# A hand-written step list after its first 43 steps in another order (attention into a GELU layer, 1 core)

## The chip, the cores and the metric

One core of one Trainium2 chip. The metric is the device time of one launch in microseconds (us); lower is better. The kernel runs alone on its core, and the granted TensorE clock is 1.000 throughout the profiled execution.

## The reference

The first half is a cross-covariance attention over channels, the second a GELU layer on its output. Cut to what matters:

```python
# q, k, v: (4, 6080, 256) float32; w_in (256, 2048), w_out (2048, 256)
qn = q / (norm(q, axis=1) + 1e-06)
kn = k / (norm(k, axis=1) + 1e-06)
s = kn.transpose(0, 2, 1) @ qn / tau        # 256 x 256 for each of 4 batches
a = softmax(s)
x = (v @ a).reshape(24320, 256)
h = x @ w_in
g = gelu_tanh(h)
out = g @ w_out
```

## The kernel before

The product `a @ w_in` is formed once for each batch (`AW`), so that the tokens need only `v @ AW`, the GELU and `@ w_out`. The tokens are cut into 48 blocks of up to 512 (12 for each batch, the twelfth of each batch has 448). All work beyond a first stretch for batch 0 is cut into small steps, and the order of these steps is written out by hand: `ORDER` is a list of 48 strings, the program walks through it from left to right, and each step puts its instructions at the end of the in-order queue of its engine. A step `M5A-2` in string n works on block n-2; no step is moved by a scheduler.

What the steps of one block n are:

- `g0`..`g7` (TensorE, L521) multiply v by a pair of column blocks of AW into a PSUM tile `h` that is one of two pairs of banks; `G0`..`G7` (ScalarE, L531) apply the GELU to it and write bfloat16. Four matmuls of 512 columns for each `g`.
- Up to three *sets* w0, w1, w2 replace two such pairs each by seven half-size products (a Strassen-Winograd scheme): `w0m1`..`w0m7` on TensorE (`small`, L604, two matmuls of 256 columns each) write two PSUM tiles, `qp` (which shares the two pairs of banks with `h`) and `rb`. Between them stand `w0y5` (ScalarE, L623, copies half of `qp` to SBUF), `w0cq` (ScalarE, L620, copies `rb` into the other half of `qp`), `w0ap` and `w0ax` (VectorE, L625 and L628, sums of `rb` and that copy), and three GELUs `w0Gq`, `w0Gr`, `w0Gx` (L630, L635, L638). `w0m6` adds to `rb` and so waits for `w0cq`; `w0m3` and `w0m7` wait for `w0ap`; `w0m4` waits for `w0ax`.
- The second layer is a Winograd scheme as well: `M1A`, `M1B` to `M7A`, `M7B` (TensorE, `product`, L736, four matmuls of 256 columns each) accumulate in the halves r and p of one PSUM tile `rp`, of which there is one. `T1a`, `T2`, `T3`, `T4` (VectorE) are the sums of g that M5, M6, M7 and M4 read. `y5` (ScalarE, L759) copies p to SBUF, then `cq` (ScalarE, L794) copies r to p, and M2 and M6 go on from there; then `c11` (VectorE, L774) transposes r into the output tile, `ap` (VectorE, L798) writes p plus the copy into r, and M3 and M7 go on; `ax` (L765) reads p before M4; `c12` and `c21` read both halves before M1 of the next block.
- In between lies the attention of the next batch: `lq`, `lk`, `lv` (loads on GpSimd's queue, each behind the last matmul issued so far), `lt` (a transposing load on SyncE's queue, which also holds the stores), `row0`.. (TensorE, L253), `qsq`, `ksq` (squares, on ScalarE or for some on VectorE, L192 and L194), `f1`..`f3`, `sp`, `sa`, and the chain from `gc` to the copies `ac0`..`ac7` and the sums `SW0`..`SW2` for the sets. `pF0`, `pS1` and the like prepare `w_out` once, early.

So within one block there are two places where ScalarE reads half of a PSUM tile and writes the same tile (`y5` and `cq` of the block, `y5` and `cq` of each set) and one where VectorE does (`c11` and `ap`). The pairs as the code writes them, the block's first, then the set's (`hc` is half the block's columns, `c` all of them):

```python
elif what == "y5":    # keep(): SBUF <- ACCS[n, "p"], on nc.scalar
    keep(n, "p", "y5")
elif what == "cq":
    nc.scalar.activation(ACCS[n, "p"][:, :hc], ACCS[n, "r"][:, :hc], AF.Copy)
...
if what == "cq":
    nc.scalar.activation(qp(n, i)[:, 0, :c], RB[n, i][:, :c], AF.Copy)
if what == "y5":
    YW[n, i] = set_buffer(n, i, "y")
    nc.scalar.activation(YW[n, i][:, :c], qp(n, i)[:, 1, :c], AF.Copy)
```

Of the kernel before, what the change touches and what calls it, by code (L numbers as in the profile page):

```python
# [18 lines left out]
def kernel(  # L19
# [1004 lines left out]
    """g0 lq+2 w2m4-1 w1ax-1 w1m4-1 row1-1 w1Gr-1 c11-2 ap-2 M3A-2 T4-2 M3B-2 sp-2 sa-2 vs M7A-2
    M7B-2 ax-2 w2Gr-1 G0 w0m1 w0m5 w0cq w0y5 row2-1 g3 G3 w0m6 c12-2 row0 ksq-1 w0ap f1-1 M4B-2
    M4A-2 c21-2 row3-1 w1m5 w0m7 w1Gx-1 lk+2 w1y5 w1m1 w1cq w0m2 w0m3 w0Gq w0ax w0Gx T2-1 M1A-1
    M5B-1 w1m6 w1ap w0m4 w0Gr M1B-1 T4-1 w2m5 w2y5 M5A-1 y5-1 cq-1 w1m7 w2m1 w2cq w1m2 row4 w1m3
    w1Gq M6B-1 w1ax M2B-1 w1m4 M2A-1 vs+1 M6A-1 T3-1 w2m6""",
    """w0m5 w1Gr-1 row3-1 row5-3 w0m1 w1Gx-1 row4-3 ksq-1 c11-2 ap-2 M7A-2 w0cq w0y5 M7B-2 w2ap-1
    c22-3 w2m3-1 w2m2-1 w2m7-1 w2Gq-1 qsq+1 f2-2 f3-2 w2ax-1 row2-1 w0m6 w0ap M3B-2 M3A-2 c12-2  # L1030
    ax-2 lk w2Gx-1 w2m4-1 w2Gr-1 row2-3 g0 G0 lt+2 T1a-1 T2-1 w0m7 qsq-1 w0m2 w0m3 M4A-2 row0-3
    M4B-2 c21-2 lv+3 w0ax sp-2 sa-2 g3 M1A-1 G3 w0Gq c22-2 f1-1 M1B-1 M5A-1 M5B-1 y5-1 T3-1 f2-1
    cq-1 row1-1 w1m1 w1m5 w0m4 w2m5 w1cq w0Gr T4-1 row0+1 M6B-1 w1y5 w1m6 M6A-1 w2m1 M2A-1 M2B-1
    w2y5 w0Gx w1ap w1m3 w1m2 w1m7 f3-1 row3+1 w2cq w2m6 row2+1 qsq c11-1 ap-1 M3B-1 M7A-1 w1ax
    w1m4 w1Gx w1Gq w2ap M7B-1 ax-1 w1Gr ksq row1 w2m7 w2m3 w2m2 lk+6 w2ax M3A-1 w2Gq M4B-1 w2Gx
    vs+1 w2m4 sp-1 sa-1 lt+3 M4A-1 c21-1 row2 row5-1""",
# [4 lines left out]
    """w0m1 vs c11-2 w1m7-1 g7-1 G7-1 ap-2 M3A-2 w1ax-1 lt+2 w0m5 T1a-1 w0cq M7A-2 M7B-2 M3B-2 f1-1
    w0y5 ax-2 w0m6 w0ap w1m4-1 g0 w1Gx-1 M4B-2 T2-1 w1Gr-1 w0m7 w0ax row4-1 f2-1 lv+3 w0m3 G0
    w0m2 M4A-2 w0Gq w1m1 c12-2 w1m5 c21-2 w1cq row5-1 w1y5 w0m4 w0Gr row4-4 row1-1 gc M1A-1 w0Gx
    w1m6 M1B-1 f3-1 T4-1 w1ap M5B-1 M5A-1 vs+1 w2m5 y5-1 sp-1 sa-1 pow w1m2 w1m3 T3-1 w1m7 cq-1
    M6A-1 lv+4 lt+3 M2B-1 M2A-1 M6B-1 w1Gq w1ax w2y5 w2m1 w2cq w1m4 w1Gr c11-1 ap-1 kf kr c22-2
    g3 G3 w2m6 M7B-1 w2ap M7A-1 ax-1 krp lq+4""",
    """w0m1 S1 S0 w2m7-1 T1a-1 w1Gx-1 w0m5 w0cq w0y5 w2m3-1 M4A-2 lq+4 w2m2-1 w2Gq-1 M4B-2 w2ax-1
    w0m6 th1 th0 w0ap M3A-2 c22-2 M3B-2 c12-2 c21-2 w2Gx-1 w2m4-1 g0 dn w0m7 w0m3 w0m2 T2-1
    M1B-1 rc3 w2Gr-1 lt+3 G0 M1A-1 M5A-1 M5B-1 rc1 g3 w0Gq g4 w0ax y5-1 cq-1 G3 T3-1 rc2 G4
    M2B-1 w1m1 w1m5 rc0 M6B-1 w0m4 M6A-1 w1cq w1m6 w1y5 w1ap lk+4 ksq+3 M2A-1 g7 w1m7 w0Gx c11-1  # L1050
    ap-1 w1m2 w1m3 M7A-1 eT M3A-1 w0Gr w1Gq w1ax lv+4 G7 vs+1 M7B-1 rsum+1 rs+1 w1m4 M3B-1""",
# [19 lines left out]
    w2m6 w1ax w1m4 w1Gr w1Gx M7B-1""",
    """w0m5 M3A-2 w0m1 T4-2 w0cq w2ap-1 T1a-1 ax-2 w2m3-1 w2m2-1 w2m7-1 row4+2 w2Gq-1 w2ax-1 ksq
    row0-1 w0y5 w0m6 w0ap M4A-2 w2Gx-1 M4B-2 w2m4-1 w2Gr-1 c21-2 g3 w0m7 G3 c12-2 lt+2 w0m2 w0m3
    M1B-1 M5B-1 M5A-1 w0Gq w0ax w0Gx w0m4 T2-1 vs+1 w0Gr T4-1 w1m1 w1m5 row0+2 w1cq lv+3 M1A-1
    row4-2 sp-2 sa-2 row5-2 y5-1 cq-1 w1y5 w1m6 w1ap w2m5 w2y5 M6B-1 w2m1 w2cq M6A-1 M2B-1
    row1-2 f1-1 f2-1 qsq row3-1 w2m6 w2ap w1m3 w1m2 w1Gq w1m7 w1ax w1Gx M2A-1 c11-1 ap-1 lv+6
    f3-1 row1+2 w2m3 w2m7 w2ax w1m4 w1Gr T3-1 w2m2 w2Gq g0 M3A-1 G0 M3B-1 w2Gx c12-1 c22-2 lt+3""",
    """g3 G3 w0m5 w0m1 T1a-1 T2-1 M7B-2 w2m4-1 M7A-2 ax-2 w0y5 w0cq g0 w2Gr-1 w0m6 w0ap row0-3 row1
    row3+1 sp-2 sa-2 f1-1 G0 qsq M4B-2 M4A-2 c21-2 c22-2 lk+2 w1m5 w1y5 w1m1 w0m7 w0m3 w0ax w0m2
    M1B-1 M5B-1 vs+1 w1cq w1m6 w0Gq w1ap w0Gx w0m4 w0Gr M1A-1 M5A-1 y5-1 cq-1 w2m5 w1m7 w1m3  # L1080
    w1m2 T3-1 w2m1 w2y5 w2cq M2A-1 w1Gq w1ax M6B-1 w1m4 T4-1 w1Gr w2m6 w2ap lt+4 w1Gx lk+3 M6A-1
    M2B-1""",
    """w0m5 w0y5 w0m1 w0cq w2m3-1 w2m2-1 c11-2 ap-2 f2-2 w2m7-1 row5 w2Gq-1 M3A-2 w0m6 w2ax-1
    w2Gx-1 M3B-2 f3-2 w0ap row5-1 w2m4-1 M7A-2 ksq-1 w0m7 M7B-2 w0ax w2Gr-1 ax-2 g0 qsq c12-2
    lq+1 vs+1 w0m4 w0Gr row0-2 w0m2 T1a-1 w0m3 lq+2 M4A-2 M4B-2 c21-2 G0 sp-2 row3-1 w1m1 w1m5
    row3-2 row2-1 f1-1 w0Gq M1A-1 M1B-1 f2-1 f3-1 w1cq sa-2 w1m6 M5A-1 M5B-1 row4-1 sp-1 w2m5
    w1y5 w1ap ksq c22-2 lt+2 w1m3 w1m2 w1m7 sa-1 y5-1 cq-1 w2m1 M2B-1 M2A-1 T2-1 M6A-1 M6B-1
    lk+3 T3-1 w1Gq w0Gx g3 w2y5 w2cq w2m6 w1ax w1m4 w1Gx row5-2 w1Gr row3+1 G3 c11-1 ap-1 M7B-1
# [193 lines left out]
```

## Time and profile before

| | us |
|---|---|
| median of 3 runs | 697.04 |
| lowest, highest | 696.74, 697.15 |
| the profiled execution, its own time | 696.96 |
| its span, first to last instruction | 695.2 |

Outside the span lie 1.76 us (696.96 less 695.2). The views are read so: a *page* has busy times by engine and the costliest groups of instructions; the *chain* is the work that ended last, followed back from the end, and its pieces give a start, a length and a count of instructions; the *timeline* gives each instruction's start and length in us, with equal neighbours merged under a count (x4). The length of a matmul in the trace is modelled and is longer than the distance to the next one's start, so holds of TensorE are read from starts. PE is TensorE, PEld its weight loads, ACT ScalarE, DVE VectorE, POOL GpSimd, SP SyncE.

### The profile page before, as it was taken

What the parts mean: (1) busy time and instruction counts of PE and PEld (TensorE: products, weight loads), DVE (VectorE), ACT (ScalarE), POOL (GpSimd) and SP (SyncE); (2) the same over time, 40 slices, a digit from 0 to 9 for tenths busy, and PEclk for the clock granted to TensorE, in tenths of its full rate; (3) what the DMA queues carried; (4) which work ended last, traced back from release to release, by engine and by line L of the source; (5) the groups of instructions that cost most, each with busy time, mean ns of one, the idle gap of its engine ahead of it and who ended that gap; (6) DMA issues with size and microseconds to landing.
All of it is one profiled execution on the core that took longest, in us unless ns stands there. A gap on an engine that the chain in (4) does not pass through costs nothing.

```text
span 695.2 us, 14706 instructions
## 1 busy us (share of the span) xinstructions
PE 677.7 (97%) x5707; PEld 543.8 (78%) x5707; DVE 630.0 (91%) x1111; ACT 624.0 (90%) x945; POOL 74.5 (11%) x135
## 2 busy tenths in 40 slices
...
GB/s 241 207 270 133 180 151 115 110 118 69 151 128 117 110 90 144 131 115 94 173 83 132 95 110 132 64 107 101 46 92 61 117 77 85 99 47 64 70 62 58
DMA packets 161463, 79.08 MB, mean 114 GB/s; under 512 B 148449, under 2 KB 152161, under 8 KB 160673
## 3 DMA queue, kind: packets, MB, share of 16 engines
...
## 4 chain that ended last, share of the span: by engine, by line
PE 82%; ACT 8%; DVE 4%; DMA 4%; issue 1%; DVEq 0%; POOL 0%; ACTq 0%; POOLq 0%
PE rp L736 36%; PE h L521 15%; PE rb L604 13%; PE qp L604 10%; PE G L253 4%; DMA t<-in_k_dram 3%; PE awp L454 1%; DMA t<-in_q_dram 1%; ACT g L531 1%; ACT yw L623 1%; ACT qp L620 1%; ACT g L635 1%; ACT sq L192 1%; PE o L748 1%; ACT g L630 1%
## 5 line engine op out<-in xcount | busy, mean ns | idle before, releaser
L736 PEld LDWEIGHTS <-wcomb 128*128 128x128 bf16 x2632 | 256.0, 98 | 43.9 <-issue 2.4
L736 PE MATMUL rp<-t,wcomb 128*128 128x256 bf16 (+1 forms) x1504 | 209.3, 272 | 0.1
L736 PE MATMUL rp<-g,wcomb 128*128 128x256 bf16 (+1 forms) x1128 | 160.2, 272 | 0.3 <-ACT rp L794 0.2
L531 ACT ACTIVATE g<-h 128x1024 bf16<-128x1024 f32 (+1 forms) x136 | 137.6, 1017 | 11.6 <-PE h L521 11.0
L630 ACT ACTIVATE g<-qp 128x1024 bf16<-128x1024 f32 (+1 forms) x124 | 125.0, 1015 | 9.3 <-PE qp L604 8.8
L521 PE MATMUL h<-vT,aw 128*128 128x512 bf16 (+1 forms) x456 | 115.8, 377 | 0.2 <-ACT g L630 0.2
L604 PEld LDWEIGHTS <-sw 128*128 128x128 bf16 x992 | 96.3, 98 | 23.9 <-issue 2.4
L625 DVE TENSOR_TENSOR qp<-rb,yw 128x512 f32<-128x512 f32 (+1 forms) x124 | 85.3, 689 | 13.0 <-PE rb L604 5.3
L604 PE MATMUL rb<-tv,sw 128*128 128x256 bf16 (+1 forms) x496 | 93.0, 271 | 0.4
L628 DVE TENSOR_TENSOR xw<-rb,yw 128x512 f32<-128x512 f32 (+1 forms) x124 | 83.4, 675 | 2.0 <-PE rb L604 1.3
L521 PEld LDWEIGHTS <-aw 128*128 128x128 bf16 x544 | 52.8, 98 | 39.2 <-DVE aw L362 0.6
L604 PEld LDWEIGHTS <-aw 128*128 128x128 bf16 x744 | 72.4, 98 | 13.3 <-issue 0.2
L620 ACT ACTIVATE qp<-rb 128x512 f32<-128x512 f32 (+1 forms) x124 | 71.9, 583 | 8.3 <-PE rb L604 2.9
L638 ACT ACTIVATE g<-xw 128x512 bf16<-128x512 f32 (+1 forms) x124 | 77.4, 627 | 1.7 <-DVE xw L628 1.5
L635 ACT ACTIVATE g<-rb 128x512 bf16<-128x512 f32 (+1 forms) x124 | 72.7, 595 | 3.6 <-PE rb L604 3.2
L623 ACT ACTIVATE yw<-qp 128x512 f32<-128x512 f32 (+1 forms) x124 | 73.0, 596 | 2.4 <-PE qp L604 0.7
L192 ACT ACTIVATE sq<-t 128x1536 bf16<-128x1536 bf16 (+4 forms) x49 | 64.5, 1335 | 6.2 <-DMA t<-in_q_dram 6.0
L774 DVE STREAM_TRANSPOSE ot<-rp 128x256 f32<-128x256 f32 (+1 forms) x141 | 59.0, 433 | 6.2 <-PE rp L736 5.2
L253 PE MATMUL G<-t 128*128 128x256 bf16 (+1 forms) x352 | 60.6, 277 | 0.6 <-DMA t<-in_k_dram 0.6
L711 DVE TENSOR_TENSOR t<-g,t 128x2048 bf16<-128x2048 bf16 (+1 forms) x47 | 56.7, 1207 | 0.5
L707 DVE TENSOR_TENSOR t<-g,t 128x2048 bf16<-128x2048 bf16 (+1 forms) x47 | 56.3, 1198 | 0.5
L709 DVE TENSOR_TENSOR t<-g 128x2048 bf16<-128x2048 bf16 (+1 forms) x47 | 56.5, 1203 | 0.0
...
## 6 DMA issues: line engine op xcount, KB each, us to landing
...
vb<-in_v_dram POOLq DMA_DIRECT2D x41, 256.0 KB, 4.2
t<-in_q_dram POOLq DMA_DIRECT2D x21, 384.0 KB, 6.0
t<-in_k_dram POOLq DMA_DIRECT2D x21, 384.0 KB, 5.9
...
```

Of the source, the lines that this page charges most:

```text
L253: nc.tensor.matmul(G[b][:, jc, :], lhsT=qt[:np_, r, jc * 128 : jc * 128 + 128], rhs=kt[:np_, r, :], start=first and jc == 0, stop=jc == 1, ...
L521: mm = nc.tensor.matmul(hp[:, u, :cols], lhsT=AW[b][:, cc, fc * 128 : fc * 128 + 128], rhs=vt_tiles[n][:, cc, :cols], start=cc == 0, stop= ...
L531: nc.scalar.activation(gs(n)[:, 2 * p : 2 * p + 2, :cols], HP.pop((n, p))[:, :, :cols], AF.Gelu_apprx_tanh)
L604: GATE[0] = nc.tensor.matmul(acc[:, u * hc : u * hc + hc], lhsT=lhs[:, u * 128 : u * 128 + 128], rhs=rhs, start=m in (1, 5) and u == 0, st ...
L620: nc.scalar.activation(qp(n, i)[:, 0, :c], RB[n, i][:, :c], AF.Copy)
L623: nc.scalar.activation(YW[n, i][:, :c], qp(n, i)[:, 1, :c], AF.Copy)
L625: nc.vector.tensor_add(qp(n, i)[:, 1, :c], RB[n, i][:, :c], YW[n, i][:, :c])
L628: nc.vector.tensor_add(XW[n, i][:, :c], RB[n, i][:, :c], YW.pop((n, i))[:, :c])
L630: nc.scalar.activation(gs(n)[:, 2 * pa : 2 * pa + 2, :c].rearrange("p u (t x) -> p t u x", t=2), QP.pop((n, i))[:, :, :c].rearrange("p t ( ...
L635: nc.scalar.activation(gs(n)[:, 2 * pb : 2 * pb + 2, :hc], two(RB.pop((n, i))[:, :c]), AF.Gelu_apprx_tanh)
L638: nc.scalar.activation(gs(n)[:, 2 * pb : 2 * pb + 2, hc:c], two(XW.pop((n, i))[:, :c]), AF.Gelu_apprx_tanh)
L736: nc.tensor.matmul(ACCS[n, acc][:, :hc], lhsT=wcomb[:, w, fc, :], rhs=x, start=first and k == 0, stop=k == 3, skip_group_check=True)
```

## The change

The list `ORDER` is replaced from its 44th step on (the first string, 38 steps, and five steps of the second stay). All 3887 steps are the same ones, with the same tiles and shapes and so the same instructions; only their sequence differs, and with it where the 48 strings are cut. Of the diff, the early part and two strings:

```diff
-    """g0 vtr0-1 vtr1-1 lt+2 lv+3 G0 g3 G3 M1A-1 g2 lq+1 G2 g1 pF0-1 lk+1 lt+3 pS1-1 G1 pA12-1
-    M1B-1 M5B-1 M5A-1 g6 g7 pF1-1 pS2-1 T3-1 y5-1 cq-1 M2B-1 T2-1 M6A-1 M6B-1 pS4-1 vs+1 M2A-1
-    c11-1 ap-1 row5 G6 G7 pNA-1 g5 pS3-1""",
+    """g0 vtr0-1 vtr1-1 lt+2 lv+3 pF0-1 M1A-1 g3 G0 SW1-1 lq+1""",
+    """w0m1 G3-1 pS1-2 g2-1 G2-1 M1B-2 T2-2 pA12-2 g1-1 G1-1 M5A-2 M5B-2 y5-2 cq-2 g6-1 pF1-2 G6-1
+    pNA-2 pS3-2 lk row2-1 g7-1 G7-1 M2A-2 pS2-2 pA21-2 M6A-2 M6B-2 T3-2 pS4-2 M2B-2 g4-1 G4-1
...
-    """g0 G0 lq+1 w0m5 M7A-2 w0m1 f1-2 f2-2 f3-2 M7B-2 ax-2 c22-2 row4-3 row5-2 sp-2 sa-2 w0cq w0m6
-    row0-2 w0y5 w0ap w2m5-1 row0-3 f1-1 w1Gx-1 w2m1-1 M4B-2 w0m7 w0ax w2y5-1 w2cq-1 w0m2 w0m3
...
+    """w0m5 w0m4-1 M3B-2 w1ax-1 w1Gx-1 lv+4 w1m4-1 w1Gr-1 f1-2 M3A-2 w0Gr-1 row5-4 row4-4 w0m1 w0cq
+    f2-2 f3-2 g0 w0y5 row4-3 G0 w0m6 sp-2 T1a-1 M7B-2 lk+1 row1-2 row3-2 lt+2 w2m5-1 w0ap w2y5-1
+    sa-2 w0m7 ksq w2m1-1 w2cq-1 ksq-1 w0ax w0m2 w0m3 w0Gq row2-2 row2-3 row5 lq+1 w2m6-1 M7A-2
...
```

Counted in each engine's queue, the second of a pair stands directly behind the first, that is, the read of a PSUM tile directly ahead of the write to it:

| pair | of | before | after |
|---|---|---|---|
| `y5`, `cq` of a block (ScalarE) | 47 | 45 | 39 |
| `y5`, then `cq` of a set (ScalarE) | 124 | 63 | 57 |
| `c11`, `ap` of a block (VectorE) | 47 | 46 | 41 |

Where a set has `cq` first, `y5` stands directly behind it 41 times before and 45 times after. The queues of SyncE and GpSimd hold the same loads and stores in another sequence.

More of the change, by code (lines that the diff above doesn't have):

```diff
@@ L1025 @@
[L1025 to L1036, printed above, removed]
@@ L1043 @@
[L1043 to L1048, printed above, removed]
@@ new lines @@
+    w2cq w1m4 w1Gr T4-1 g3 w1Gx krp S1+1 G3 S0+1 th0+1 w2m6 w2ap M3B-1 M7A-1 M7B-1 ax-1 c22-1""",
+    """w0m1 lt+2 w0m5 w2m7-1 w2ax-1 w2m3-1 w0cq T1a-1 w0y5 w2m2-1 w2Gq-1 M4B-2 M4A-2 lk+3 w0m6
+    M3A-2 w0ap th1 c12-2 w2Gx-1 c21-2 w2m4-1 g0 dn w0m7 w0m3 w0m2 T2-1 M1B-1 rc3 w2Gr-1 lt+3 G0
+    M1A-1 M5A-1 M5B-1 rc1 g3 w0Gq g4 w0ax y5-1 cq-1 G3 T3-1 rc2 G4 M2B-1 w1m1 w1m5 rc0 M6B-1
+    w0m4 M6A-1 w1cq w1m6 w1y5 lk+4 w1ap ksq+3 M2A-1 g7 w1m7 w0Gx c11-1 ap-1 w1m2 w1m3 M7A-1 eT
+    M3A-1 w0Gr w1Gq w1ax lv+4 G7 vs+1 M7B-1 rsum+1 rs+1 w1m4 M3B-1""",
@@ L1071 @@
[L1071 to L1088, printed above, removed]
@@ L1238 @@
[L1238 to L1242 removed]
+    w1Gx T3-1 g3 G3 c11-1 ap-1 row3 M3B-1 M3A-1 w2ap w2m3 w2m2 M7A-1 w1Gr""",
@@ new lines @@
+    vs+1 sp-2 ax-2 M4B-2 qsq+1 T2-1 w0m6 sa-2 M4A-2 w0ap row5+1 row4+1 w1m5 w1m1 w0m3 w0m7 w0m2
+    w1y5 w1cq c21-2 c12-2 c22-2 M1B-1 M5B-1 M5A-1 w0ax w1m6 w0Gq T4-1 lt+3 w0Gx w0m4 w0Gr row4-1
+    M1A-1 w1ap T3-1 f1-1 y5-1 cq-1 row1+1 w1m7 w1m3 w2m5 w1m2 w2y5 row3 w2m1 M6A-1 M2A-1 M2B-1
+    w1ax w1m4 ksq w2cq w2m6 w2ap M6B-1 w1Gq""",
+    """w0m5 row5-1 c11-2 w1Gr-1 ap-2 w0m1 w1Gx-1 w2m7-1 w2ax-1 w0y5 T1a-1 w2m3-1 w2m2-1 w0cq row2-1
+    w2Gq-1 M3B-2 qsq-1 lt+3 w0m6 w0ap f2-2 f3-2 w2Gx-1 w2m4-1 w2Gr-1 M3A-2 M7A-2 M7B-2 ax-2 g0
@@ new lines @@
+    G0 w0m7 w0m2 row0-2 c12-2 w0ax w0Gx w1m1 M4A-2 w0m4 w0Gr T3-1 M4B-2 c21-2 lq+1 w1m5 w1cq
+    w1y5 row3+2 w0m3 lk+1 sp-2 sa-2 f1-1 w0Gq M1A-1 w1m6 M1B-1 w1ap M5A-1 M5B-1 y5-1 row5+2 cq-1
+    w1m3 w1m2 w1m7 w1Gq w2m5 w2y5 T2-1 row5-2 f2-1 f3-1 M2B-1 M6A-1 ksq sp-1 w1ax M6B-1 sa-1
+    M2A-1 w2m1 T4-1 g3 c11-1 ap-1 row4+2 w2cq w2m6 w1m4 M3B-1 c22-2 lk+3 w1Gx M3A-1 w2ap w2m3
+    w2m2 w1Gr vs+1 f1 M7A-1 G3 w2m7 w2ax w2Gq""",
+    """w0m5 w0m1 w0y5 w0cq M7B-2 g0 c12-2 ax-2 G0 T1a-1 w2Gx-1 w2m4-1 w0m6 w0ap M4B-2 M4A-2 w2Gr-1
@@ new lines @@
+    lv+9 sa-1 row2 w2m1 T3-1 w2cq M2B-1 M2A-1 row5+1 f1 w2m6 lq+4 w2ap w1y5 w1m6 w1ap M6A-1
+    ksq+1 M6B-1 ksq+2 row3+1 w2m7 w2m3 w1m7 w2ax row0+2 w2Gx w1m3 row1+2 w1m2 w1Gq w2m2 w2m4
+    w2Gq c11-1 ap-1 M3A-1 M3B-1 w1ax w1m4 M7A-1 w1Gr vs+1""",
+    """w0m5 lq+2 M7B-2 ax-2 vs+1 w0y5 w0m1 w0cq w1Gx-1 g0 G0 w0m6 M4B-2 M4A-2 w0ap c21-2 c12-2 w0m3
+    w2Gr-1 w0m2 w0m7 w0Gq w0ax w0Gx g3 G3 T1a-1 T2-1 M1B-1 T3-1 w0m4 w0Gr w2m5 lk+2 w2y5 M1A-1
+    M5B-1 M5A-1 y5-1 w1m5 lv+3 cq-1 w1m1 w2m1 row4+3 row5+3 T4-1 row5+1 M2A-1 w2cq w1y5 w2m6
@@ new lines @@
+    w2m3 w2m2 M3A-1 M3B-1 c12-1 aw7 w2Gq ax-1 ac7 w2Gx T3 w2m4""",
+    """g0 w2Gr-1 G0 M4A-2 M4B-2 c21-2 c22-2 w0m5 w0y5 w0m1 w0cq w1m4-1 w1Gr-1 g3 M1B-1 G3 M1A-1
+    lv+5 w0m6 M5A-1 M5B-1 y5-1 cq-1 T2-1 SW1-1 w1m5 w0ap w1m1 vs+1 w2m1 w0m7 w0ax w1cq w1y5
+    SW2-1 w0m3 w0m2 w0Gq M6A-1 w1m6 w1ap M2B-1 w0Gx M6B-1 M2A-1 c11-1 ap-1 w2m5 w2cq w2y5 w0m4
+    w1m7 lt+2 w0Gr w1m2 w1m3 w1Gq w1ax w2m6 w2ap M7B-1 M7A-1 w1Gx M3A-1""",
+    """w0m1 T4-2 w2m3-1 w2m2-1 w2Gq-1 ax-2 w2m7-1 w2ax-1 w1m4-1 w0m5 w0cq M4B-2 M4A-2 M3B-2 w0y5 g3
@@ new lines @@
+    T1a-1 w0m6 w2Gx-1 c12-2 w1Gr-1 c21-2 w2m4-1 M1A-1 w2Gr-1 c22-2 G3 M5A-1 M5B-1 w0ap w0m2 y5-1
+    w0m3 g0 w0Gq w0m7 G0 M1B-1 cq-1 T2-1 T4-1 w2m5 w2m1 w1m1 w0ax w0m4 w1m5 M6A-1 T3-1 M6B-1
+    w2y5 lv+8 w2cq w2m6 vs+1 M2B-1 w2ap w1cq w1m6 w1y5 w1ap M2A-1 c11-1 w2m3 lt+2 w2m7 ap-1 w0Gx
+    w2ax w0Gr w2m2 w1m2 w1m3 w1Gq T1a w1m7 w1ax w2Gq""",
+    """w0m1 M3A-2 M7A-2 w0m5 w0y5 w0cq M7B-2 M3B-2 g0 w1Gx-1 ax-2 w0m6 c12-2 G0 lv+2 M4B-2 w0ap
+    w1m4-1 M4A-2 w0m2 w1Gr-1 c22-2 c21-2 w1m5 w0m7 w0ax w2Gx-1 T3-1 w0m3 w1m1 lv+4 M1A-1 lt+2
@@ new lines @@
+    M1B-1 w1y5 w1cq M5B-1 w0Gq w1m6 w1ap w2m4-1 M5A-1 w2Gr-1 y5-1 cq-1 w2m5 w0m4 w1m7 w1m3 w1m2
+    w2m1 w2y5 w2cq M2A-1 T2-1 M6A-1 M6B-1 w1Gq w0Gx w2m6 w1ax w1m4 w1Gr T4-1 w0Gr g3 M2B-1 G3
+    w2ap w2m7 w2m3 w2m2 w2Gq""",
+    """w0m1 w1m1 vs w0m5 w0cq w0y5 c11-2 ap-2 M3A-2 M7A-2 M3B-2 w2ax-1 w0m6 T1a-1 w0ap w1m5 w1cq
+    w1y5 M7B-2 ax-2 w2m4-1 w2Gr-1 w0m3 w0m2 w1m6 c12-2 w1ap w0m7 M4B-2 w0ax M4A-2 c21-2 w2m1
+    w1m2 w2Gx-1 w1Gx-1 T2-1 w1m3 w0Gq w1m7 M1A-1 w1ax M5A-1 M5B-1 w1Gq lt+3 M1B-1 w0Gx y5-1 cq-1
@@ new lines @@
+    M3A-1 M3B-1 c12-1 ax-1 lt+3 w0Gx T1a""",
+    """w0m1 w0m5 w1m4-1 g3 w2Gx-1 w0cq w0m6 w0y5 w0ap M4A-2 w2m4-1 G3 w1Gr-1 M4B-2 c21-2 w0m2 w0m3
+    w1m5 w1m1 M1A-1 w2Gr-1 M1B-1 M5A-1 w0Gq M5B-1 w0m7 w2m5 w2m1 T2-1 T4-1 w1y5 w1cq w1m6 y5-1
+    cq-1 M2A-1 w2y5 w2cq M6A-1 w0ax w0m4 w0Gx w1ap w1m2 w1m3 w2m6 vs+1 M2B-1 w1Gq w2ap w1m7
+    M6B-1 w1ax w2m7 w2m3 w2m2 w1Gx w2Gq c11-1 ap-1 g0 G0 M3B-1 T3-1 w2ax w0Gr M3A-1 c22-2 T1a""",
+    """g0 w0m5 M7A-2 G0 w0m1 w0cq w0y5 M7B-2 ax-2 w2m4-1 c12-2 g3 w0m6 M4B-2 w0ap w2Gx-1 M4A-2
@@ new lines @@
+    c21-2 G3 w2Gr-1 w1m4-1 w1Gr-1 w0m7 w0ax w0m2 w0m3 w0Gq w1m5 w1y5 M1A-1 M5A-1 T3-1 w1m1 M5B-1
+    M1B-1 w2m5 T2-1 w1cq w1m6 w1ap T4-1 y5-1 w0m4 w2m1 cq-1 M2B-1 M6A-1 w1m7 M2A-1 w2y5 w1ax
+    w2cq w2m6 w0Gr w0Gx w1Gx M6B-1 w1m2 w1m4 w1Gr w1m3 w1Gq""",
+    """w0m1 w2ap-1 w2m7-1 w2m3-1 w2m2-1 lt+2 w2Gq-1 c11-2 ap-2 c22-3 M7A-2 M3A-2 vs w0m5 w0cq w0y5
+    T1a-1 M7B-2 M3B-2 ax-2 w2ax-1 g0 G0 w0m6 w0ap M4A-2 M4B-2 c21-2 w2Gx-1 w2m4-1 w2Gr-1 c12-2
+    w0m2 vs+1 w0m3 w0Gq g3 G3 M1A-1 M1B-1 M5A-1 M5B-1 y5-1 cq-1 w1m1 w0m7 w2m5 w1m5 w2m1 T2-1
```

356 lines of the change are left out of this document (167 added, 189 removed).

## The prediction, written before the change was run

> **What bounds the kernel now.** First the page, for which engine carries the time:
>
> ```profile
> span 695.2 us, 14706 instructions
> PE 677.7 (97%) x5707; PEld 543.8 (78%) x5707; DVE 630.0 (91%) x1111; ACT 624.0 (90%) x945; POOL 74.5 (11%) x135
> PE 82%; ACT 8%; DVE 4%; DMA 4%; issue 1%; DVEq 0%; POOL 0%; ACTq 0%; POOLq 0%
> ```
>
> TensorE is busy 97% of the span and is 82% of the chain; ScalarE and VectorE follow at 90 and 91%. The change leaves every instruction as it is, so it can only move time in which TensorE is held. The busy share does not show these holds, because a matmul's length in the trace is longer than its distance to the next. So next the pieces of the chain, which show how fast TensorE goes when nothing holds it, and the windows, which part the stretch that changes (from about 50 us) from the one that doesn't:
>
> ```profile
> 53.64 1.73 PE h L521 x8
> 55.37 1.75 PE rp L736 x16
> ...
> 71.46 1.90 PE rp L736 x16
> 676.58 1.77 PE rp L736 x16
> 50.00:690.80 640.80, 639.65 (x5390) 517.47 (x5388) 601.71 (x1062) 597.27 (x919) 55.72 (x101) 1.00 0.62 104
> ```
>
> Sixteen matmuls of 256 columns take 1.75 us, 0.109 each; eight of 512 columns take 1.73, 0.216 each. The pieces at 71.46 and 676.58 are 0.15 and 0.02 longer than sixteen should be: TensorE was held there. Between these two, the first and the last after 50 us, I find 78 steps held by over 0.02 us, by comparing all starts with these distances; together 8.4 us. So of the 640.8 us after 50 us some 632 are matmuls at full pace, and 8.4 us is all that an order can win there. How one hold arises shows the timeline:
>
> ```profile
> 430.02 0.38 ACT L759 ACTIVATE y<-rp 128x256 f32<-128x256 f32 x1
> 430.44 0.37 ACT L794 ACTIVATE rp<-rp 128x256 f32<-128x256 f32 x1
> 430.72 0.59 ACT L623 ACTIVATE yw<-qp 128x512 f32<-128x512 f32 x1
> 430.86 1.03 PE L736 MATMUL rp<-t,wcomb 128*128 128x256 bf16 x8
> 431.34 0.58 ACT L620 ACTIVATE qp<-rb 128x512 f32<-128x512 f32 x1
> 431.97 0.49 PE L604 MATMUL rb<-tv,sw 128*128 128x256 bf16 x3
> ```
>
> These are y5 and cq of a block, then y5 and cq of a set. The third starts 0.09 us before the second ends (430.44 + 0.37 = 430.81), as neighbours on ScalarE mostly do. Each cq starts 0.03 to 0.04 after its y5 has ended: both touch one PSUM tile, and the write waits until the read is quite finished. The pair costs 0.12 us more than strangers. The eight matmuls should have ended their issue at 430.86 + 0.87 = 431.73; w1m6 of block 28 starts at 431.97, 0.05 after the cq has ended. Held: 0.24 us, the price of the two pairs.
>
> VectorE has the same thing:
>
> ```profile
> 615.11 0.69 DVE L625 TENSOR_TENSOR qp<-rb,yw 128x512 f32<-128x512 f32 x1
> 615.71 0.68 DVE L628 TENSOR_TENSOR xw<-rb,yw 128x512 f32<-128x512 f32 x1
> ...
> 630.39 0.45 DVE L774 STREAM_TRANSPOSE ot<-rp 128x256 f32<-128x256 f32 x1
> 630.88 0.43 DVE L798 TENSOR_TENSOR rp<-rp,y 128x256 f32<-128x256 f32 x1
> ```
>
> L628 starts 0.09 before L625 ends; ap (L798) starts 0.04 after c11 (L774) ends: 0.12 again.
>
> **The change part by part.** I sort the 78 holds by the instruction that ended about 0.05 us before. Of each kind here stand the first and the last, the releaser and the step held:
>
> ```profile
> 147.61 0.58 ACT L620 ACTIVATE qp<-rb 128x512 f32<-128x512 f32 x1
> 148.25 0.27 PE L604 MATMUL rb<-tv,sw 128*128 128x256 bf16 x1
> 640.16 0.58 ACT L620 ACTIVATE qp<-rb 128x512 f32<-128x512 f32 x1
> 640.79 0.27 PE L604 MATMUL rb<-tv,sw 128*128 128x256 bf16 x1
> ...
> 124.56 0.37 ACT L794 ACTIVATE rp<-rp 128x256 f32<-128x256 f32 x1
> 124.98 0.27 PE L736 MATMUL rp<-t,wcomb 128*128 128x256 bf16 x1
> 676.02 0.37 ACT L794 ACTIVATE rp<-rp 128x256 f32<-128x256 f32 x1
> 676.44 0.27 PE L736 MATMUL rp<-g,wcomb 128*128 128x256 bf16 x1
> ...
> 152.53 1.03 ACT L630 ACTIVATE g<-qp 128x1024 bf16<-128x1024 f32 x1
> 153.62 0.38 PE L521 MATMUL h<-vT,aw 128*128 128x512 bf16 x1
> 600.67 1.02 ACT L630 ACTIVATE g<-qp 128x1024 bf16<-128x1024 f32 x1
> 601.74 0.27 PE L604 MATMUL qp<-tv,sw 128*128 128x256 bf16 x1
> ...
> 70.96 0.43 DVE L798 TENSOR_TENSOR rp<-rp,y 128x256 f32<-128x256 f32 x1
> 71.45 0.27 PE L736 MATMUL rp<-t,wcomb 128*128 128x256 bf16 x1
> 631.37 0.27 PE L736 MATMUL rp<-g,wcomb 128*128 128x256 bf16 x1
> ```
>
> A: the set's cq ahead of m6, 23 holds, 2.7 us. B: the block's cq ahead of M2 or M6, 15 holds, 2.15 us. C: a GELU ahead of a bank's next writer, 17 holds, 1.5 us. D: VectorE, 18 holds, 1.6 us (ap alone 11 and 0.95, the last at 631.37 behind the L798 of 630.88). The rest, five, are 0.4 us. In 44 of the 78 the releaser is the second of such a pair, directly behind the first: 5.3 us, of which pairs at 0.12 can explain 3.9.
>
> The order does not part most pairs: directly behind each other stand 45 + 63 + 46 = 154 before and 39 + 57 + 41 = 137 after. What it wins must come from where TensorE has more to do meanwhile. For this I go through both lists with the durations of the rows: a place counts when ScalarE or VectorE, in its queue's order, needs longer from a step released by TensorE to the step that TensorE waits for (0.20 us into the engine, 0.05 out, neighbours overlapping by 0.09 or apart by 0.03) than the matmuls that stand between on TensorE. In the old list these are 96 places, many sharing one late stretch, and 59 are holds in the trace; in the new list 58. By kind:
>
> - A: 35 places before, 14 after. 2.7 us shrink to 2.7 x 14/35 = 1.1: 1.6 won.
> - B: 17 before, 8 after. 2.15 shrink to 1.0: 1.1 won. From M5 to M2 or M6 an idle ScalarE needs 0.20 + 0.39 + 0.03 + 0.37 + 0.05 = 1.04 us, ten matmuls; with less between stand four blocks before (8, 41, 43, 46) and two after.
> - C: 29 before, 11 after. 1.5 shrink to 0.6: 0.9 won.
> - D: 8 before and 23 after, but of the 23 eleven share one late stretch and four another, so that 8 stretches stand against 8. The largest shortfalls of the stretches add up to 0.6 us before and 1.05 after: 0.5 lost.
>
> The one stretch of eleven needs a look, since there a step is newly queued ahead of others: in block 5 two K squares stand between w0ap and w0ax.
>
> ```profile
> L194 DVE TENSOR_TENSOR sq<-t 128x1536 bf16<-128x1536 bf16 x10 | 9.3, 938 | 0.0
> L670 DVE CAST wcomb<-wf 128x1024 bf16<-128x1024 f32 x1 | 0.7, 694 | 0.0
> vb<-in_v_dram POOLq DMA_DIRECT2D x41, 256.0 KB, 4.2
> t<-in_k_dram POOLq DMA_DIRECT2D x21, 384.0 KB, 5.9
> vT<-vb SPq DMA_TRANSPOSE x45, 4.6
> ```
>
> Two squares are 1.88 us on VectorE, and w0ax, w2ap and w2ax are queued behind them; w0m4, w2m3, w2m4 and M1 wait for those. TensorE has 3.4 us of matmuls from w0m6 to w0m4, which covers most; I find up to 0.31 us missing, which is in D. If VectorE comes 1 us late to w0ap, nothing covers it, and the place costs that 1 us.
>
> At nothing I cost the rest. Loads: the shortest stretch of matmuls from a K or Q load to its first use falls from 9.6 us to 8.1 (K of the first chunk for batch 2), against 5.9 to landing and about 0.6 to issue; without that cover ScalarE would wait the difference. lt of block 10 stands right behind its lv and keeps SyncE's queue, with the stores behind it, for 4.2 us; from any lt to the first matmul on it are 7.4 us at least (5.5 before), against 4.6. The early preparation of w_out moves about a block later: S1 (0.69 us) has 2.2 us of matmuls to M5. Taken off ScalarE and VectorE are 17 x 0.12 = 2 us, hidden but for what is counted.
>
> Sum: 1.6 + 1.1 + 0.9 - 0.5 = 3.1 us less. The profiled execution took 696.96 with a span of 695.2; the median is 697.04, 0.1 from it. Forecast: 697.0 - 3.1 = 693.9 us.
>
> A rule weighed: the Trainium skill, VectorE: DVE Perf Modes, section The DRAIN you can't avoid, has each VectorE operation followed by a flush that no chaining avoids; that section adds that an operation that is not held starts earlier. The rows above differ from its first half: 0.09 early beside 0.04 late. By the flush alone the five parted c11, ap pairs would save nothing, 5 x 0.12 = 0.6 us at most, and the time would be 694.5.
>
> **The rivals.** *No change.* ScalarE and VectorE have 597 and 602 us of work in the 641, and that is not less. A hold taken from m6 may return at the next step that waits for the same late engine, since 137 pairs stay. For: the 2 us taken off are 0.2% of their work. Against: 44 of 78 holds have a pair's price in them, and the places fall in three kinds at once. If all return but those 2 us on one of the two engines at half weight, 1 us is won: 696.0; none, 697.0. I take 696.6.
>
> *VectorE becomes the bound (slower).* With 23 places behind VectorE instead of 8, and 1.88 us of squares in the worst, its lateness may not die between them. If each of the 23 costs 0.24 us, the second largest shortfall that I found, 5.5 us are lost against the 3.6 won by A, B and C: 698.9. It decides from 3.6/23 = 0.16 us a place, and from 0.22 the kernel is slower by over 1.4 us. Against: the 15 that share two stretches are one hold each, as D has it, and VectorE's total is no larger.
>
> **How the numbers follow.** 0.2% is 1.4 us, about what a measurement of this kernel can tell from no change. The forecast's own range: if all 5.3 us of the 44 pair holds go and D costs its 0.5, 4.8 us are won (692.2); half of A, B and C with D as it is gives 1.3 (695.7). The forecast has 0.66, nearly all faster. No change has 0.18, of it 0.04 beyond 1.4 us. Slower has 0.16, of it 0.01 within. Faster: 0.70, same 0.15, slower 0.15. The range reaches down to 691.7, the 5.3 us without D's loss, and up to 698.0, which takes in no change and the milder part of slower, leaving out some 0.2.
>
> **What would show it.** Right: after 50 us the holds add up to 5 to 6 us; fewer cq (L620, L794) end 0.05 us ahead of a held matmul; the timeline still shows 0.03 behind each direct pair and overlaps elsewhere. Wrong: as many holds, now behind GELUs or ap and ax; or several tenths at w0m4, w2m3 and w2m4 near 110 to 125 us; or a load that ends a wait of ScalarE. A new order with holds over 8.4 us makes the prediction wrong.

## The result and the profile after

The changed kernel takes 694.0 us (median of six executions, 693.62 to 694.84) beside 696.88 for the kernel before on the same chip: ratio 0.9959, 95% interval 0.9946 to 0.9972. The forecast was 693.9. Its profiled execution took 694.25 us. Here and below the fences hold only the lines that are spoken of. From the page, the line of the span, the line of the busy times and the first line of the chain, then the window after 50 us:

```profile
span 692.5 us, 14625 instructions
PE 671.3 (97%) x5643; PEld 543.7 (79%) x5707; DVE 630.7 (91%) x1111; ACT 624.0 (90%) x945; POOL 74.4 (11%) x135
PE 88%; DMA 5%; issue 3%; ACT 2%; POOL 0%; DVE 0%; DVEq 0%; POOLq 0%
50.00:688.10 638.10, 633.49 (x5325) 517.16 (x5385) 602.54 (x1062) 597.04 (x919) 55.58 (x100) 1.00 0.66 105
```

ScalarE and VectorE are as busy as before, to 0.7 us. In the chain ACT falls from 8% to 2% and DVE from 4% to 0: it passes fewer waits of TensorE for these two. They have not gone, since by the table below about half of the time of these waits (A to D), 4.0 of 8.0 us, is left. (64 matmul records are missing; their starts follow from the weight loads, of which all 5707 are there.) Counted as in the prediction, 51 holds are left after 50 us, 5.5 us in all, against 78 and 8.4. By kind, predicted and found:

| held step waits for | before, us (holds) | predicted after | after, us (holds) |
|---|---|---|---|
| A: the set's cq | 2.7 (23) | 1.1 | 0.63 (10) |
| B: the block's cq | 2.15 (15) | 1.0 | 0.80 (6) |
| C: a GELU | 1.5 (17) | 0.6 | 0.93 (10) |
| D: VectorE | 1.6 (18) | 2.1 | 1.68 (17) |
| rest | 0.4 (5) | 0.4 | 1.46 (8) |

Won by the holds: 2.85 us; by the times of the two profiled executions: 696.96 - 694.25 = 2.71.

The place of the prediction's first timeline, y5 and cq of block 28's set w1 and the w1m6 behind, in the changed kernel's timeline:

```profile
429.13 0.60 ACT L623 ACTIVATE yw<-qp 128x512 f32<-128x512 f32 x1
429.56 0.60 PE L736 MATMUL rp<-g,wcomb 128*128 128x256 bf16 x4
429.76 0.58 ACT L620 ACTIVATE qp<-rb 128x512 f32<-128x512 f32 x1
430.00 0.60 PE L736 MATMUL rp<-t,wcomb 128*128 128x256 bf16 x4
430.44 0.38 PE L253 MATMUL G<-t 128*128 128x256 bf16 x2
430.65 0.38 PE L604 MATMUL rb<-tv,sw 128*128 128x256 bf16 x2
```

The pair stands as it did: cq starts 0.03 us after y5 ends (429.73 to 429.76). But w1m6 does not wait. Its cq ends at 430.34, TensorE is busy until 430.65, last with the two matmuls of a row, and 0.26 us are to spare. From the last matmul that feeds the pair to w1m6 there are 2.73 us of matmuls where there were 1.64.

Over all places it is mixed. I take all 44 where the second of a pair had released a hold, and measure the matmul time from the start of the last feeding matmul to the start of the waiting step, less the hold. Its median grew from 1.42 to 1.64 us for a set's cq and from 1.42 to 1.52 for ap. For a block's cq it grew from 1.20 to 1.64 counted from M5, which feeds y5, and stays at 1.20 counted from the later of M5 and M1, which feeds cq. Place by place, counted from the later one, 23 of the 44 have more matmul time ahead than before, 6 the same and 15 less. At the 15 the holds fall too, from 2.1 to 0.6 us: there the engine needs less time from that matmul to the end of its write, 0.49 us less in the median. So slack, the matmul time less what the engine needs, grew from both sides. Of the 44, nine are parted in the new order (1.05 us of holds, now none) and 35 are not (4.3 us, now 1.2). That sorts the gain; causes are asked for below.

What the prediction did not have is in the last row of the table: 0.86 us at row0 of block 2. The groups of line 253 between 55 and 70 us, of the changed kernel and of a second profiled execution of the same kernel, with what ended the idle time:

```profile
L253 PE MATMUL G<-t x4: 269/271/273, 61.9 to 64.1; 128*128 128x256 bf16 x4
  DMA t<-in_k_dram: 0.7, 1
...
54.80 0.53 POOL L98 DMA_DIRECT2D t<-in_k_dram  x1 [3.56 <-PE h L521]
```

```profile
L253 PE MATMUL G<-t x4: 272/273/273, 61.8 to 63.3; 128*128 128x256 bf16 x4
```

In the first the K load, issued at 54.80 (GpSimd's timeline), landed at 63.98 and TensorE waited; in the second it was issued at 54.78 and landed at 62.24, and the row ran at 63.15 without a wait.

### The profile page after: what moved, and what is told of

Read it like the earlier page. It is cut to its first block, busy times and chain, and to the rows that moved or that the text cites. A ratio compares the mean times of both kernels' runs of the same rounds, so it can differ in the third digit from the quotient of the medians.

```text
span 692.5 us, 14625 instructions
## 1 busy us (share of the span) xinstructions
PE 671.3 (97%) x5643; PEld 543.7 (79%) x5707; DVE 630.7 (91%) x1111; ACT 624.0 (90%) x945; POOL 74.4 (11%) x135
## 4 chain that ended last, share of the span: by engine, by line
PE 88%; DMA 5%; issue 3%; ACT 2%; POOL 0%; DVE 0%; DVEq 0%; POOLq 0%
PE rp L736 39%; PE rb L604 15%; PE h L521 14%; PE qp L604 11%; PE G L253 5%; DMA t<-in_k_dram 4%; DMA t<-in_q_dram 1%; PE awp L454 1%; PE o L748 1%; ACT g L630 0%; ACT yw L623 0%; POOL t L98 0%; ACT qp L620 0%; ACT g L638 0%; PE ss L235 0%
## 5 line engine op out<-in xcount | busy, mean ns | idle before, releaser
L521 PE MATMUL h<-vT,aw 128*128 128x512 bf16 (+1 forms) x406 | 111.8, 376 | 2.6
L253 PE MATMUL G<-t 128*128 128x256 bf16 (+1 forms) x352 | 58.3, 276 | 1.3 <-DMA t<-in_k_dram 1.3
L711 DVE TENSOR_TENSOR t<-g,t 128x2048 bf16<-128x2048 bf16 (+1 forms) x47 | 56.7, 1206 | 0.7
L709 DVE TENSOR_TENSOR t<-g 128x2048 bf16<-128x2048 bf16 (+1 forms) x47 | 56.5, 1202 | 0.5 <-ACT g L638 0.4
L696 DVE TENSOR_TENSOR t<-g 128x2048 bf16<-128x2048 bf16 (+1 forms) x47 | 56.4, 1200 | 0.1
```

Of the source, the lines that this page charges most:

```text
L253: nc.tensor.matmul(G[b][:, jc, :], lhsT=qt[:np_, r, jc * 128 : jc * 128 + 128], rhs=kt[:np_, r, :], start=first and jc == 0, stop=jc == 1, ...
L521: mm = nc.tensor.matmul(hp[:, u, :cols], lhsT=AW[b][:, cc, fc * 128 : fc * 128 + 128], rhs=vt_tiles[n][:, cc, :cols], start=cc == 0, stop= ...
```

## The experiments

Three theories. P: a pair's 0.12 us is what makes the engine late, and parting pairs brought the gain. S (called O in the first expectations): the gain is slack, told there as more matmuls ahead of the step that waits. L: loads, which the prediction costed at nothing, set what an execution adds on top. "Pair" means read and write directly behind each other.

### Pairs parted in the kernel before (three kernels)

The edit swaps neighbours on one engine; matmuls stay in place among themselves. One of the 37 swaps, VectorE's ap of block 1:

```diff
-    T4-1 c22-2 M6B-1 M2B-1 G3 g4 qsq vs+1 lk+2 c11-1 ap-1 lq+3""",
+    T4-1 c22-2 M6B-1 M2B-1 G3 g4 qsq c11-1 vs+1 lk+2 ap-1 lq+3""",
```

> The order of before, in which 37 of the 44 pairs whose second instruction released a hold of TensorE are parted: one neighbouring instruction of the same engine is put between read and write, or the read goes one place up; no matmul step is moved against another. The holds of these 37 add up to 4.38 us; at 0.12 us a pair at most 3.3 us of it is the pair's. Theory P (the 0.12 us of a pair is what makes ScalarE or VectorE late): 2.0 to 3.3 us less than before, about 694.3, and the 37 holds shrink by 0.1 each. Rival O (the change won by where it puts its matmuls, so that steps that wait stand further from what they wait for; pairs are incidental): within 0.7 us of before, the holds stay or return at the next step.

> The order of before, in which 37 pairs are parted in the same way that released no hold of TensorE; the 44 that did are kept. Theory P: a pair that no matmul waits for costs only engine time, which counts where the engine is late later in the same stretch: 0 to 1.2 us less than before, about 696.3. Rival T (engine time counts wherever it is saved, 37 x 0.12 = 4.4 us taken off two engines): as much as in the kernel with the 37 held pairs parted, 2.0 to 3.3 us less, about 694.3. Rival O: within 0.7 us of before.

> The order of before with all pairs parted that a swap of neighbours can part: 154 become 32. Theory P: the 3.3 us of the held pairs, and up to 1.2 us from the others: 4 to 5 us less than before, about 692.5, below the changed kernel. Rival O: within 0.7 us of before, 697. In between, 694 to 696, the holds return behind other instructions of the same engines (GELU, ax, c21), and the parting pays once a stretch, not once a pair.

Measured: 708.67 us (ratio to before 1.0171, 1.0158 to 1.0184), 713.56 (1.0241, 1.0228 to 1.0254) and 748.38 (1.0740, 1.0726 to 1.0753). Every theory was wrong: none had a loss. The timeline of the first kernel at the swap shown:

```profile
70.25 0.45 DVE L774 STREAM_TRANSPOSE ot<-rp 128x256 f32<-128x256 f32 x1 [1.11 <-PE rp L736]
70.62 0.38 DVE L558 TENSOR_TENSOR tv<-vT 128x512 bf16<-128x512 bf16 x1
71.04 0.29 DVE L560 TENSOR_TENSOR tv<-vT,tv 128x256 bf16<-128x256 bf16 x1
71.37 0.29 DVE L561 TENSOR_TENSOR tv<-vT,tv 128x256 bf16<-128x256 bf16 x1
71.58 0.42 DVE L798 TENSOR_TENSOR rp<-rp,y 128x256 f32<-128x256 f32 x1
72.05 1.03 PE L736 MATMUL rp<-t,wcomb 128*128 128x256 bf16 x8 [0.76 <-DVE rp L798]
```

Where c11 and ap were 0.10 apart (70.86 to 70.96 before), the three sums of vs now stand between, ap starts 0.88 after c11's end, and M7B is held 0.92 us instead of 0.16. What parts a pair takes 0.4 to 1.5 us to run and saves 0.12. At the 44 places the holds grew from 5.3 to 8.7 us in the first kernel; in all it has 20.3 us of holds, the third 60.2. So "another instruction between" is no gain by itself, and where the write is urgent it is a loss of that instruction's length. Most of the new holds in the first kernel, 8.6 of 11.9 us, stand at other steps. The largest, 1.06 us at w1m4 of block 26, waits for w1ax, which a swap had put behind c11. A swap thus changes two waits, and these kernels do not price the pair alone.

### The K load issued earlier

```diff
-    """w0m1 G3-1 pS1-2 ... pNA-2 pS3-2 lk row2-1 g7-1 ...
+    """w0m1 lk G3-1 pS1-2 ... pNA-2 pS3-2 row2-1 g7-1 ...
```

> The changed kernel with one DMA issued earlier: lk of block 2, which lands 9.2 us after its issue at 54.8 us and holds the first matmul of row0 for 0.86 us at 64.0 us, is put 20 steps ahead, right behind w0m1. If that hold is TensorE's own loss by a late load: the hold is gone and the time is 0.9 us less than the changed kernel, about 693.1. Rival: TensorE is then held at the next steps by ScalarE or VectorE, which had caught up during the wait: 0 to 0.3 us won, 694.

Measured: 696.62 us, twelve executions from 694.23 to 705.0; both expectations missed. In the profiled one (694.73) the load left at 50.95, 3.9 us earlier, and landed 13.5 us later at 64.4: row0 was held 1.64 us. By the windows the share of the DMA engines is 1.18, 1.31 and 1.10 in the three stretches of 5 us from 50 to 65, so other loads are under way all the time, and in this execution the earlier issue brought no earlier landing. By the Trainium skill, DMA: Bandwidth & Descriptors, section Issuing engines are not separate DMA queues, all transfers run on the same 16 engines and interleave. That fits these shares, but no run here takes the other loads away. Five of the twelve executions took 700.8 us and more; none of them was profiled, and why they are so long stays open.

### The changed kernel once more

> The changed kernel once more, beside the three that follow. 694.0 us if its time is as steady as the first six executions (693.6 to 694.8). A rival: like the kernel with the earlier lk (694.2 to 705.0 over twelve executions) it has executions at 700 and more, which six executions did not show.

Measured: 694.34 us, five executions, 693.25 to 695.25; ratio to before 0.9960 (0.9949 to 0.9972). None at 700. Its profiled execution, at 693.25, is the one above without a wait at row0: a us less than the first profile, 0.86 of it that wait.

### The pair's price without the pair

Nothing is moved. Twenty instructions that the change had parted from their reads wait for the instruction just ahead of them:

```diff
-                step(m[1], n + {None: 0, "+": 1, "-": -1}[m[2]] * int(m[3] or 0))
+                s = (m[1], n + ...); step(*s); "%s.%d" % s in WAITS and wait_for_last(*s)
```

> The changed kernel with its order untouched; 20 instructions (14 cq, 6 ap) that stood directly behind their pair's first in the kernel before and stand apart now are given a wait for the instruction just ahead of them on their engine, so that each starts 0.03 us behind its end instead of 0.09 before it: the pair's price without the pair. Theory P (the parting brought the gain): up to 20 x 0.12 = 2.4 us, of it 1 to 2 us more than the changed kernel, 695 to 696. Theory S (the gain is slack: matmuls were moved so that a wait for ScalarE or VectorE has more matmuls ahead of it, and 35 of the 44 holding pairs lost their hold unparted): 0 to 0.3 us more, 694.2.

Measured: 694.63 us (694.03 to 696.86), 0.29 more than the changed kernel beside it, within the scatter of both. The wait did take effect; ScalarE's timeline at cq of block 14, with the wait and without:

```profile
247.91 0.59 ACT L620 ACTIVATE qp<-rb 128x512 f32<-128x512 f32 x1
248.53 0.37 ACT L794 ACTIVATE rp<-rp 128x256 f32<-128x256 f32 x1
```

```profile
246.87 0.59 ACT L620 ACTIVATE qp<-rb 128x512 f32<-128x512 f32 x1
247.38 0.35 ACT L794 ACTIVATE rp<-rp 128x256 f32<-128x256 f32 x1
```

The second instruction starts 0.03 behind the end of the first instead of 0.08 before it. It starts 0.03 behind at 16 of the 20, on both engines; 15 of these had started before the end. Between the two traces the holds of eight steps behind the added waits grew, by 0.76 us in all. (M6A of block 0, ahead of the first added wait, is held 0.54 us more, behind VectorE's work on `w_out`.) So of 20 x 0.12 = 2.4 us at most 0.8 reach TensorE in this order: S holds, and P has a small part.

### The parted pairs joined again

The read is moved down to stand directly ahead of the write, for w2 of block 6 past three GELUs:

```diff
-    y5-1 cq-1 M2B-1 M6B-1 T4-1 M6A-1 w1ax f2-1 w2y5 w1m4 w0Gr w1Gq w1Gr T3-1 M2A-1 c11-1 ap-1
-    w2m1 w2cq""",
+    y5-1 cq-1 M2B-1 M6B-1 T4-1 M6A-1 w1ax f2-1 w1m4 w0Gr w1Gq w1Gr T3-1 M2A-1 c11-1 ap-1 w2m1
+    w2y5 w2cq""",
```

> The changed kernel with 17 of its 20 parted pairs joined again: the read is moved down to stand directly ahead of the write, what stood between comes earlier. The write then ends 0.12 us later, the instruction from between up to 0.6 us earlier, the read's result later by as much. Theory P: 1 to 2 us more than the changed kernel, 695 to 696. Theory S: 0 to 0.5 us more, 694.2.

Measured: 697.18 us (696.82 to 698.67), ratio to before 1.0004 (0.9995 to 1.0012): 2.8 us more than the changed kernel, above both expectations. ScalarE's timeline and m6 of that set, joined, then in the changed kernel:

```profile
127.01 0.60 ACT L635 ACTIVATE g<-rb 128x512 bf16<-128x512 f32 x1 [0.36 <-PE rb L604]
127.50 0.59 ACT L623 ACTIVATE yw<-qp 128x512 f32<-128x512 f32 x1
128.76 0.38 PE L604 MATMUL rb<-tv,sw 128*128 128x256 bf16 x2 [0.26 <-ACT qp L620]
```

```profile
124.96 0.59 ACT L623 ACTIVATE yw<-qp 128x512 f32<-128x512 f32 x1
127.54 0.58 ACT L620 ACTIVATE qp<-rb 128x512 f32<-128x512 f32 x1
128.17 0.38 PE L604 MATMUL rb<-tv,sw 128*128 128x256 bf16 x2
```

With the read early, only cq lies between the last GELU and m6. Joined, ScalarE idles 0.36 us ahead of that GELU and then has read and write to do: m6 is held 0.42 us. The largest holds that came new or grew are 0.2 to 0.4 us each, more than the pair's price. The position of the read in the queue counts, and what it can be done ahead of. How much of the 2.8 us is that and how much mere damage to a tuned list, this kernel does not part.

### The middle of the list alone

At some steps both orders have done the same set of steps, so the lists can be spliced there. By the first trace the change is behind at first: `rsum` of block 11 (step 851) starts at 185.68 us before and 186.24 after; M5B of block 34 at 525.30 and 523.03; M6B of block 43 at 642.35 and 638.62. (In the second profile, which has no wait at row0, `rsum` starts at 185.38, ahead of before.)

```diff
-steps 1-850 and 3586-3887: the order of the change
+steps 1-850 and 3586-3887: the order of before
```

> Steps 1 to 850 and 3586 to the end in the order of before, those between in the order of the change (at both cuts the same steps are done in both orders). By the two traces the change is 0.55 us behind at step 850 (186 us), 2.3 us ahead at step 2911, 3.7 us ahead near 3586 and 2.75 us ahead at the end. If each stretch keeps its own gain: 0.55 and 0.95 us less than the changed kernel, about 692.5. Rival: the stretches hand on their lateness (loads that come earlier or later, buffers), and the gain of the middle shrinks to what the changed kernel has: 694.

Measured: 693.5 us, nine of eleven executions between 693.24 and 694.57, two at 698.0; ratio to before 0.9962 (0.9947 to 0.9977). Of the two gains expected, the first, 0.55 us, is the wait at row0, which the old order of that stretch does not have. The second was misread. Behind the second cut the changed kernel loses nothing: the last matmul ahead of that cut starts at 638.00 us before and 635.16 after, 2.84 apart, and the last matmul of all is 2.97 apart. M6B of block 43 seemed further ahead because it has eight matmuls (0.87 us) fewer ahead of it in the new list. The middle carries the gain: ahead of the first cut, between the cuts and behind the second the holds are 1.4, 6.6 and 0.4 us before and 1.3, 3.0 and 0.3 in the second profile of the changed kernel. Its profiled execution (694.57) has a wait that no other profile shows, on VectorE's timeline and then TensorE's:

```profile
344.48 0.39 DVE L558 TENSOR_TENSOR tv<-vT 128x448 bf16<-128x448 bf16 x1 [1.13 <-DMA vT<-vb]
346.54 0.69 DVE L625 TENSOR_TENSOR qp<-rb,yw 128x512 f32<-128x512 f32 x1
347.29 0.38 PE L604 MATMUL rb<-tv,sw 128*128 128x256 bf16 x2 [0.75 <-DVE qp L625]
```

The transposing load for block 23 came late, VectorE stood, and w1m7 of block 22 was held 0.92 us. In the changed kernel, at the same step, there was no wait.

### Slack given and slack taken

First the kernel before, with one matmul step moved ahead of the held one at 15 places:

```diff
-    ... w1y5 M6A-1 M6B-1 T4-1 w2m6 vs+1 w2ap M2B-1 w1m6 w1ap
+    ... w1y5 M6A-1 M6B-1 T4-1 M2B-1 w2m6 vs+1 w2ap w1m6 w1ap
```

> The order of before, pairs untouched. At 15 of the 38 places where a cq releases a held m6, M2 or M6, one later step of 2 or 4 matmuls (0.22 or 0.44 us), which waits for nothing, is put ahead of the held step; the 15 holds add up to 1.70 us. Theory S (a hold is a lack of matmuls ahead of the step that waits): the 15 holds go, 1.0 to 1.7 us less than before, about 695.5, less what the delayed steps' own readers lose. Rival P (the pair's price makes ScalarE late, which a few matmuls do not cure): the holds return at the next step that waits for ScalarE, within 0.4 us of before.

Measured: 698.26 us (697.99 to 700.06), ratio 1.0018 (1.0008 to 1.0028), 1.4 us more. Of the 15 holds 14 are gone and one is 0.03 us: that half of S is shown. But 9.8 us of holds stand there instead of 8.4. VectorE's and TensorE's timelines around w2 of block 29, whose m6 (the first two of the four matmuls at 446.95) is no longer held:

```profile
446.95 0.60 PE L604 MATMUL rb<-tv,sw 128*128 128x256 bf16 x4
447.44 0.70 DVE L625 TENSOR_TENSOR qp<-rb,yw 128x512 f32<-128x512 f32 x1 [0.83 <-PE rb L604]
448.19 0.38 PE L604 MATMUL qp<-vT,sw 128*128 128x256 bf16 x2 [0.20 <-DVE qp L625]
```

ap starts later, and w2m3 is held 0.37 us, where it was not held before. The same step of the chain holds w2m3 of block 37 (0.37), w0m7 of 39 (0.37) and w1m2 of 8 (0.27). This is the return that the prediction's first rival spoke of, one step further down the set. At these places a single step later only moved the wait to the next helper of the chain.

Then the changed kernel, with one matmul step taken from ahead of the waiting one at 11 places:

```diff
-    w1y5 w1cq c21-2 c12-2 c22-2 M1B-1 M5B-1 M5A-1 w0ax w1m6 w0Gq T4-1 ...
+    w1y5 w1cq c21-2 c12-2 c22-2 M1B-1 M5B-1 w0ax w1m6 M5A-1 w0Gq T4-1 ...
```

> The changed kernel, pairs untouched. At 11 places that were held in the kernel before, are not held now and have more matmuls ahead, one neighbouring step of matmuls is taken from ahead of the waiting step and put behind it. From the changed kernel's trace the waiting steps had 0.08 to 1.07 us to spare; where a step taken away is longer than what there was to spare, a hold of the difference comes back: 6 places, 1.2 us in all. Theory S: 1.2 us more than the changed kernel, about 695.5. Rival P: pairs are as they were, so 0 to 0.3 us more, 694.3.

Measured: 695.56 us (694.7 to 697.7), 1.2 more than the changed kernel. Six holds were expected, of 0.49, 0.35, 0.13, 0.12, 0.11 and 0.02 us; found are, at the same steps, 0.50, 0.35, 0.13, none, 0.11 and 0.02. The place of the diff:

```profile
261.83 0.60 PE L736 MATMUL rp<-t,wcomb 128*128 128x256 bf16 x4
261.98 0.58 ACT L620 ACTIVATE qp<-rb 128x512 f32<-128x512 f32 x1
262.62 0.38 PE L604 MATMUL rb<-tv,sw 128*128 128x256 bf16 x2 [0.18 <-ACT qp L620]
```

Four matmuls fewer, 0.44 us, 0.09 to spare: held 0.35, with no pair changed. The time has the load's scatter in it (ratio to before 0.9979, 0.9968 to 0.9990, where the changed kernel has 0.9960); the holds have not.

### The load's place exchanged, and the best version

```diff
-    lk+1 T3-1 lq+1 w0m6 w0ap M4B-2 M4A-2 c21-2 row0 c12-2 ...
-    lt+2 w0m1 w1m6 w0cq row0-3 row4-1 row1-2 ...
+    lk+1 T3-1 lq+1 w0m6 w0ap M4B-2 M4A-2 c21-2 row0-1 c12-2 ...
+    lt+2 w0m1 w1m6 w0cq row0-2 row4-1 row1-2 ...
```

> The changed kernel with two steps exchanged that add rows to the same sum: the early place of row0 of block 2, whose K load was still on its way in two of three profiles of this order (held 0.86 us) and had landed in a third (no hold), gets row0 of block 1, long loaded, and the other way round. Theory L (the executions differ by when that load lands): the time stays near its lowest, 693.3, and most executions lie within 0.4 us of each other instead of 2. Rival: the load then holds qsq, ksq or another row of block 2 instead, and median and spread are as before, 694.3.

> As the kernel with the two rows exchanged, and lv of block 23 issued 68 steps earlier: in one execution of the spliced order VectorE waited 1.13 us at 344.5 us for the transposing load behind it, and w1m7 of block 22 was held 0.92 us. Theory L: 693.3 at the most, without single executions 1 us higher; 0 to 0.5 us below the kernel with the rows exchanged alone. Rival: the earlier lv delays lk and lq behind it on GpSimd's queue, and another load ends late: 694 or more.

Measured: 693.67 us (693.3 to 694.14), ratio to before 0.9947 (0.9932 to 0.9962), and with `lv` earlier 693.45 (692.99 to 693.63), ratio 0.9943 (0.9928 to 0.9958). The expectation miscounted: of four profiles of this order up to then (two of the changed kernel, the one with waits, the joined one) one had the wait at row0. The direction is as L has it. In these two profiles the K load took 10.8 and 10.1 us, longer than in the five others that issue it at this place, and no step from 55 to 70 us was held over 0.12 us. The executions lie within 0.84 and 0.64 us of each other, where those of the changed kernel lie within 1.2 and 2.0, and the last kernel has the lowest median of all here, 3.4 us under before (696.85 beside it) and 0.5 to 0.9 under the changed kernel's two medians. Both medians are a little above the 693.3 expected. The intervals overlap those of the changed kernel (0.9946 to 0.9972, 0.9949 to 0.9972) and each other's: the gain in time is likely but not shown, and whether the earlier `lv` adds anything can't be told.

## Why the prediction was right, and where it was not

The time, 694.0 against 693.9, and the holds, 5.5 us in the span of 5 to 6 given, came out; in the second profile, without the wait at row0, the holds are 4.6 us. That the time was met to 0.1 us is luck, as the parts below show. The way of counting was right: walk both lists with durations from rows, and count places where an engine needs longer than the matmuls cover. The experiments on slack show that this is the cause where they touched it: taking matmuls away brings back holds of the size worked out from what there was to spare, and giving them takes holds away. That the engines also come earlier is read from two traces at the 15 places with less matmul time, and no experiment tests it alone.

- A and B were under-sized as gains: 2.1 and 1.35 us won instead of 1.6 and 1.1. Scaling a kind's holds by its number of places assumed that the places left are as bad as the old ones. For A they are milder, 0.06 us a hold instead of 0.12; for B a hold is about as long as before, but six are left.
- C was over-sized: 0.6 won instead of 0.9, ten holds left of 17.
- D was to lose 0.5 and lost 0.1. The 23 places stand against 17 holds. The count was weak here: in the old list it found 0.6 us at 8 places, where the trace has 1.6 us in 18 holds. At the K squares of block 5, w2m4 is held 0.08 us where up to 0.31 was feared.
- The step that failed is "loads at nothing". The prediction named a stretch of 8.1 us at the shortest, for another K load (the first chunk for batch 2), and set it against 5.9 us, the median landing over the whole run. The load that held TensorE is the one for block 2, the second chunk for batch 1. From its issue at 54.80 to 63.16, where row0 would have started, are 8.4 us, and it took 9.2. In the kernel before it had landed after 7.8, in the second profile after 7.5. It cost 0.86 us in the first profile and nothing in the second. That it is what makes the changed kernel scatter over 2 us, where before lies mostly within 0.5, fits the kernels with the rows exchanged and is not shown beyond that. The errors cancel: A to D won 0.8 us more than forecast, the load took 0.9 back.
- The pair's 0.12 us was measured rightly and given too much weight in the argument, as "5.3 us of which pairs can explain 3.9". The price alone is worth at most 0.8 us at 20 places, and most holds went while their pairs stayed. The sum did not rest on it; the downward end of the range (691.7) did.
- The weighed rule: the Trainium skill, VectorE: DVE Perf Modes, section The DRAIN you can't avoid, says that a semaphore between neighbours costs nothing extra, as measured there on a row of copies. Three ap that followed 0.08 us before their predecessor's end start 0.03 after it when they wait for it, so on this trace it costs 0.11 to 0.12. For the time it made no difference that can be seen: ap's three holds are 0.22 us in the changed kernel and 0.24 with the waits, and the two medians, 694.0 and 694.34, do not tell 693.9 from 694.5.
- Neither rival: VectorE did not become the bound; "no change" described what happens when slack is moved by hand at single places, not this list.
